# A delta-rule attention block feeding a cosine-gated feed-forward block: the first pair of units inverted by doubling only within blocks of 16, the norms' 1e-6 added on ScalarE, and the whole order of work laid anew

## The chip, the cores and the metric

The kernel runs on one core of one Trainium2 chip. The metric is device time in microseconds (us). The kernel before took 642.42 us, the median of three runs between 641.67 and 646.46 us. One further execution was profiled: it took 642.72 us, and its span from the first to the last instruction is 640.9 us.

## What is computed

For 4 batches and 8 heads, a recurrence runs over 768 positions with a head size of 48. Then a feed-forward block with a cosine gate works on the 3072 tokens.

```python
k_n = k / (np.linalg.norm(k, axis=-1, keepdims=True) + 1e-06)
for t in range(S):
    y[:, :, t] = einsum('bhd,bhde->bhe', q[:, :, t], state)
    v_old = einsum('bhde,bhd->bhe', state, kt)
    state = state + bt * einsum('bhd,bhe->bhde', kt, vt - v_old)
x = y.transpose(0, 2, 1, 3).reshape(B * S, H * D)      # 3072 x 384
h = x @ w_in                                            # 384 x 2048
return (h * np.cos(h)) @ w_out                          # 2048 x 384
```

All numbers are float32, except the two weight matrices, which arrive as float64 and are narrowed on the chip.

## The kernel before

**Units.** The 768 positions are cut into 24 units of 32 positions (C = 32). A unit holds all 32 pairs of batch and head. Two units make a pair (`m = n // 2`), and each pair feeds one step `p` of the feed-forward block with 256 tokens.

**A unit's way through the attention block.** Keys and queries are loaded (`load`, L392) and transposed on TensorE (`turn`, L615; copied out by `turn_out`, L625; later units use a DVE transpose instead). `gram` (L648) makes the products of keys with keys and queries. `gram_keys` (L659) scales them by beta over the squared norm; for that `scale` (L578 to L586) adds 1e-6 to the norm, squares it, takes the reciprocal and multiplies, all on VectorE (DVE). The inverse of the unit's 32x32 triangular matrices is needed before its values can be solved for: `solve` (`p_u`, L935 or L941) multiplies the right side by it, `solve_out` (L953) scales the result, `update` (`p_s`, L966) and `update_out` (L974 or L976) put it into the state, `within` (`p_kq`, L983) and `within_out` (L996) make the unit's output, `features` (`p_z`, L1004) and `features_out` (L1012) turn it into columns of the feed-forward input. The next unit's `through_state` (`p_kq`, L869) and `right_side` (L886) need that state, so the units form one long chain.

**The inverse is made in three ways.**

- Pair 0 (units 0 and 1, `DOUBLED = 2`): the matrix is split into two diagonal blocks of 16 (`near_block`) and the block between them (`OFF`). `double` (L710) inverts the two blocks by repeated squaring in levels 0 to 3, which ends in `Y3`. Levels 4 and 5 then complete the inverse: `Y3` is transposed (L722), multiplied with `OFF` (level 4), copied (L717), multiplied with `Y3` (level 5), and subtracted from `Y3` (L729), which gives `WHOLE`. Each level runs in two halves (`par`) of 16 matmuls of 32x32. `solve` then uses `WHOLE` in one step.
- Pair 1 (`HALVED = 1`): only the two blocks of 16 are inverted, by column steps on GpSimd (POOL) and DVE (`invert`, L818 and L825), after a trip through DRAM (`gram_put` L772, `gram_get` L785, `put` L830, `get` L841). The solve then takes three steps: `solve_half` (`p_w`, L899), `half_out` (ScalarE, ACT, L911), `between` (`p_v`, L899), `between_out` (DVE, L919), `solve` (`p_u`, L935).
- Pairs 2 to 11: the whole matrix by column steps on POOL.

**The feed-forward block.** The weights are narrowed tile by tile: `narrow_load` (L510), `narrow_split` (ACT, L518 and L520), `narrow_shift` (DVE, L524 and L529), `narrow_add` (POOL, L533); tiles 0 to 11 are w_in, 12 to 27 are w_out. Steps p = 0 and 1 use plain products (`hidden`, L1025, eight groups of 24 matmul records per step; `output`, L1223, for p = 0). Later steps use products with fewer multiplications (`layer`, L1199, and `product`, L1281) on sums that DVE and POOL make. The gate is `hidden_turns` (ACT, L1062), `hidden_rest` (DVE, L1069), `hidden_cos` (ACT, L1078), `hidden_gate` (DVE, L1081).

**What sets the order.** Every piece of work is a task (`add`) with its dependencies. `Order.LINE` (L97) is a list of task numbers, and the tasks are issued in just that order, so each engine's queue is a fixed list. `Order.OTHER` (L58) says which tasks go to the other of two engines: loads and stores to ACT's queue instead of SP's (SyncE's), `inv`, `x_sum`, `left` and `right` to DVE instead of POOL or the other way about. A DMA waits until the DMA eight places earlier on the shared list has landed. `keep_warm` (L487) puts matmuls without use into TensorE's list where the list expects it to be idle; 36 of them are in the program.

```python
        for key in line:
            emit, deps, makes, uses = self.tasks[key]
            assert deps <= done, key
            for tag, t in makes:
                self.place[t] = free[tag].pop(0)
            emit()
```

Of the kernel before, what the change touches and what calls it, by code (L numbers as in the profile page):

```python
# [10 lines left out]
FP = mybir.dt.float32  # L11
I32 = mybir.dt.int32
U32 = mybir.dt.uint32
ALU = mybir.AluOpType
# [41 lines left out]
class Order:  # L56

    OTHER = {  # L58
        ('gram_put', 2), ('q', 3), ('gram_get', 1), ('inv', 1, 0), ('put', 1), ('gram_put',
        4), ('gram_put', 5), ('v', 7), ('v', 8), ('v', 9), ('blocks', 11, 1), ('gram_put',  # L60
        11), ('put', 5), ('v', 13), ('put', 6), ('gram_put', 15), ('gram_get', 7), ('get',
        15), ('v', 16), ('blocks', 16, 0), ('blocks', 16, 1), ('gram_put', 16), ('blocks',
        18, 1), ('k', 19), ('blocks', 19, 0), ('gram_get', 9), ('get', 19), ('gram_put',
        20), ('v', 21), ('gram_put', 21), ('put', 10), ('gram_put', 22), ('v', 23),
        ('gram_put', 23), ('gram_get', 11), ('right', 4, 4), ('left', 1, 1, 0), ('left', 1,
        3, 0), ('left', 1, 3, 1), ('store', 1, 0), ('x_sum', 2, 'd'), ('x_sum', 2, 'n'),
        ('x_sum', 2, 'm'), ('x_sum', 2, 'e'), ('x_sum', 2, 'k'), ('x_sum', 2, 'g'),
        ('x_sum', 2, 'i'), ('x_sum', 2, 'l'), ('x_sum', 2, 'f'), ('x_sum', 2, 'b0'),
        ('left', 2, 4, 1), ('left', 2, 3, 1), ('x_sum', 3, 'd'), ('x_sum', 3, 'n'),
        ('x_sum', 3, 'm'), ('x_sum', 3, 'e'), ('x_sum', 3, 'k'), ('x_sum', 3, 'g'),  # L70
        ('x_sum', 3, 'i'), ('x_sum', 3, 'l'), ('x_sum', 3, 'h'), ('x_sum', 3, 'b0'),
        ('left', 3, 4, 1), ('left', 3, 3, 1), ('x_sum', 4, 'd'), ('x_sum', 4, 'm'),
        ('x_sum', 4, 'g'), ('x_sum', 4, 'i'), ('left', 4, 3, 0), ('left', 4, 3, 1),
        ('store', 4, 0), ('x_sum', 5, 'd'), ('x_sum', 5, 'e'), ('x_sum', 5, 'l'), ('x_sum',
        5, 'h'), ('x_sum', 5, 'b0'), ('left', 5, 2, 0), ('left', 5, 4, 1), ('left', 5, 3,
        0), ('left', 5, 3, 1), ('store', 5, 0), ('x_sum', 6, 'd'), ('x_sum', 6, 'g'),
        ('x_sum', 6, 'l'), ('x_sum', 6, 'f'), ('x_sum', 6, 'b0'), ('left', 6, 1, 0),
        ('left', 6, 4, 0), ('store', 6, 1), ('x_sum', 7, 'd'), ('x_sum', 7, 'm'), ('x_sum',
        7, 'g'), ('x_sum', 7, 'i'), ('x_sum', 7, 'f'), ('x_sum', 7, 'h'), ('x_sum', 7,
        'b0'), ('left', 7, 4, 0), ('left', 7, 4, 1), ('left', 7, 3, 1), ('x_sum', 8, 'd'),  # L80
        ('x_sum', 8, 'm'), ('x_sum', 8, 'e'), ('x_sum', 8, 'k'), ('x_sum', 8, 'g'),
        ('x_sum', 8, 'l'), ('left', 8, 3, 0), ('store', 8, 0), ('store', 8, 1), ('x_sum', 9,
        'd'), ('x_sum', 9, 'm'), ('x_sum', 9, 'e'), ('x_sum', 9, 'k'), ('x_sum', 9, 'i'),
        ('x_sum', 9, 'l'), ('x_sum', 9, 'b0'), ('left', 9, 1, 0), ('left', 9, 2, 0),
        ('left', 9, 1, 1), ('left', 9, 3, 0), ('store', 9, 0), ('x_sum', 10, 'k'), ('x_sum',
        10, 'i'), ('x_sum', 10, 'l'), ('x_sum', 10, 'h'), ('x_sum', 10, 'b0'), ('left', 10,
        1, 0), ('left', 10, 1, 1), ('left', 10, 4, 1), ('left', 10, 3, 0), ('left', 10, 3,
        1), ('store', 10, 0), ('x_sum', 11, 'd'), ('x_sum', 11, 'e'), ('x_sum', 11, 'k'),
        ('x_sum', 11, 'g'), ('x_sum', 11, 'f'), ('left', 11, 1, 0), ('left', 11, 2, 0),
        ('left', 11, 1, 1), ('left', 11, 3, 0), ('left', 11, 3, 1), ('store', 11, 1),  # L90
        ('store_right', 11), ('weights', 5), ('weights', 7), ('weights', 15), ('weights',
        16), ('weights', 18), ('weights', 20), ('weights', 22), ('weights', 23), ('weights',
        25), ('weights', 27)
# [142 lines left out]
def kernel(  # L236
# [32 lines left out]
    nc = tc.nc  # L269
# [1605 lines left out]
```

## Time and profile before

| | |
|---|---|
| median of three runs | 642.42 us (641.67 to 646.46) |
| the profiled execution | 642.72 us, span 640.9 us |
| TensorE (PE) busy | 616.0 us, 96% of the span |
| DVE / ACT / POOL busy | 510.5 / 296.4 / 441.5 us |
| PE idle from 106 to 600 us | 1.25 of 494 us |
| PE idle before 106 us | 19.96 of 106 us |

An engine's busy time is the union of its instructions' times. The idle time in the last two rows is the length of the stretch less the busy time in it. One matmul of the program shows as two matmul records and two weight loads in the trace, since its numbers are float32. A wait of an engine is put down to what ended last; "issue" means that nothing in the profile explains it. Line numbers are those of the kernel before; the changed kernel's lines lie up to 17 further down.

### The profile page before, as it was taken

To read this page: it belongs to the slowest core of one execution; us is meant where nothing else is said; L and a number is where in the kernel's file an instruction comes from. 1 tells how busy PE (TensorE), PEld (TensorE's weight loads), DVE (VectorE), ACT (ScalarE), POOL (GpSimd) and SP (SyncE) were. 2 spreads that over 40 slices of the span, in tenths; PEclk is the share of its full clock that TensorE was granted. 3 is DMA by queue.
4 is the path that set the end of the run, shared out by engine and by line. 5 is a ranking of instruction groups with operands and counts; after the bars stand their busy time and mean duration, and the time that the engine had idled before them with its cause. 6 is when DMAs were issued, how large, how long until landed. Compare 5 with 4: busy or idle time off the path is not lost.

```text
span 640.9 us, 25243 instructions
## 1 busy us (share of the span) xinstructions
PE 616.0 (96%) x10688; PEld 570.7 (89%) x10688; DVE 510.5 (80%) x1049; ACT 296.4 (46%) x528; POOL 441.5 (69%) x780
## 2 busy tenths in 40 slices
PE   5877999999999999999999999999999999999997
PEld 4655877897799999999999999999999999999997
DVE  5776877998989899887898888888888786656682
ACT  3444655654334453553642544643643553545440
POOL 5435888888778788788689888886883884112231
PEclk9887999999999999999999999999999999999999
DMA  9777556563551454434536245243304202000000
GB/s 189 200 177 180 113 157 145 93 141 54 100 88 20 98 87 70 86 69 73 88 68 104 49 70 99 49 67 67 74 2 78 45 3 41 19 2 26 2 25 26
DMA packets 209369, 50.38 MB, mean 79 GB/s; under 512 B 200920, under 2 KB 204264, under 8 KB 209256
## 3 DMA queue, kind: packets, MB, share of 16 engines
q1 hardware_dynamic: 161896, 35.03, 28.7%
q10 hardware_dynamic: 47072, 13.25, 10.1%
q8 instruction: 84, 1.38, 0.9%
q0 software_dynamic: 288, 0.50, 0.4%
q14 instruction: 29, 0.24, 0.1%
HBM read 38.51 MB, written 10.22 MB: 76 GB/s over the span
## 4 chain that ended last, share of the span: by engine, by line
PE 82%; DMA 7%; DVE 4%; issue 2%; SPq 2%; POOL 1%; ACT 1%; ACTq 0%; DVEq 0%; POOLq 0%
PE p_out L1281 28%; PE p_h L1199 27%; PE p_h L1025 6%; PE p_out L1223 3%; PE p_kq L869 3%; PE p_s L966 3%; PE p_kq L983 3%; DMA kp<-in_k_dram 3%; PE p_u L941 2%; PE p_g L648 2%; PE p_h L1281 2%; PE p_z L1004 1%; DMA g_ffn<-in_moe_w_in_dram 1%; SPq L392 1%; DMA z_dr<-z 1%
## 5 line engine op out<-in xcount | busy, mean ns | idle before, releaser
L818 POOL TENSOR_TENSOR part<-z,gb 128x126 f32<-128x126 f32 (+23 forms) x321 | 146.1, 455 | 41.8 <-DMA gb<-g_dr 12.9
L825 POOL TENSOR_TENSOR z<-z,part 128x126 f32<-128x126 f32 (+23 forms) x321 | 146.9, 458 | 25.1
L1281 PE MATMUL p_out<-w_out,g_ffn 128*128 128x192 f32 x672 | 121.9, 329 | 0.6 <-DVE o L1333 0.6
L1281 PEld LDWEIGHTS p_out<-w_out,g_ffn 128*128 128x128 f32 x672 | 107.7, 190 | 2.0 <-DVE o L1333 0.9
L1078 ACT ACTIVATE turns<-turns,halfpi 128x512 f32<-128x512 f32 x96 | 68.0, 718 | 55.0 <-DVE turns L1069 43.0
L1281 PE MATMUL p_out<-w_sum,g_ffn 128*128 128x192 f32 x496 | 89.7, 329 | 0.2 <-DVE o L1333 0.2
L1199 PE MATMUL p_h<-x_sum,w_in 128*128 128x128 f32 x640 | 84.0, 277 | 0.0
L1062 ACT ACTIVATE turns<-g_ffn,quarter_turn 128x512 int32<-128x512 f32 x70 | 49.8, 719 | 66.7 <-DVE g_ffn L1216 29.5
L1281 PEld LDWEIGHTS p_out<-w_sum,g_ffn 128*128 128x128 f32 x496 | 79.6, 190 | 1.2 <-issue 0.4
L1199 PEld LDWEIGHTS p_h<-x_sum,w_in 128*128 128x128 f32 x640 | 78.8, 192 | 1.1
L1216 DVE TENSOR_TENSOR g_ffn<-g_ffn,p_h 128x512 f32<-128x512 f32 x80 | 54.2, 680 | 17.3 <-PE p_h L1199 16.4
L1069 DVE SCALAR_TENSOR_TENSOR turns<-g_ffn,turns 128x512 f32<-128x512 f32 x70 | 54.3, 783 | 13.0 <-ACT turns L1062 12.9
L996 ACT COPY y<-p_kq 32x384 f32<-32x384 f32 x96 | 45.1, 470 | 36.4 <-PE p_kq L983 30.0
L1081 DVE TENSOR_TENSOR g_ffn<-turns,g_ffn 128x512 f32<-128x512 f32 x70 | 51.9, 751 | 3.8 <-ACT turns L1078 3.7
L567 POOL TENSOR_TENSOR knrm<-ksum,halves 128x16 f32<-128x16 f32 (+1 forms) x14 | 38.4, 2745 | 22.8 <-DVE ksum L555 20.7
L1199 PE MATMUL p_h<-x_sum,in_sum 128*128 128x128 f32 x400 | 52.9, 277 | 0.0
L1199 PEld LDWEIGHTS p_h<-x_sum,in_sum 128*128 128x128 f32 x400 | 49.7, 192 | 0.8
L1333 DVE SCALAR_TENSOR_TENSOR o<-p_out,o 128x192 f32<-128x192 f32 x74 | 25.1, 351 | 29.3 <-PE p_out L1281 28.8
L1025 PE MATMUL p_h<-x_ffn,w_in 128*128 128x128 f32 x384 | 46.1, 277 | 0.0
L1025 PEld LDWEIGHTS p_h<-x_ffn,w_in 128*128 128x128 f32 x384 | 44.2, 192 | 1.4 <-issue 0.2
L1199 PE MATMUL p_h<-x_ffn,w_in 128*128 128x128 f32 x320 | 42.4, 277 | 0.0
L1297 POOL TENSOR_TENSOR g_ffn<-g_ffn,g_ffn 128x512 f32<-128x512 f32 x18 | 25.4, 1417 | 23.2 <-PE p_out L1281 19.4
(156 smaller groups left out, 1080.8 us busy)
## 6 DMA issues: line engine op xcount, KB each, us to landing
g_ffn<-in_moe_w_in_dram SPq DMA_DIRECT2D x10, 512.0 KB
gb<-g_dr SPq DMA_DIRECT2D x14, 256.0 KB
vp<-in_v_dram SPq DMA_DIRECT2D x68, 48.0 KB
g_ffn<-in_moe_w_out_dram SPq DMA_DIRECT2D x8, 384.0 KB
g_ffn<-in_moe_w_out_dram ACTq DMA_DIRECT2D x8, 384.0 KB
kp<-in_k_dram SPq DMA_DIRECT2D x120, 24.0 KB
out_dram<-o SPq DMA_DIRECT2D x14, 192.0 KB
zt<-z_dr SPq DMA_DIRECT2D x72, 32.0 KB
```

Of the source, the lines that this page charges most:

```text
L567: nc.gpsimd.tensor_tensor(out=scales[m][2][:, part], in0=sums[m, part.start][:, 0:n], in1=halves[:, 0:n], op=ALU.pow,)
L818: eng.tensor_tensor(out=part, in0=z[:, 0:rows, j, None].to_broadcast(shape), in1=a[:, j, None, j + 1 :].to_broadcast(shape), op=ALU.mult,)
L825: eng.tensor_tensor(out=behind, in0=behind, in1=part, op=ALU.subtract)
L996: nc.scalar.copy(by_parity(y[quarter(b)]), p_kq[quarter(b ^ 1), :, b % 2])
L1025: nc.tensor.matmul(p_h[:, i], w_in[:, t, (4 * k + i) * 128 : (4 * k + i + 1) * 128], xts[p][:, t, unit * 128 : (unit + 1) * 128], start=(i ...
L1062: nc.scalar.activation(turns[p, f], hidden_of(p, f), AF.Identity, bias=quarter_turn, scale=TURN)
L1069: nc.vector.scalar_tensor_tensor(out=r, in0=hidden_of(p, f), scalar=TURN, in1=t, op0=ALU.mult, op1=ALU.subtract,)
L1078: nc.scalar.activation(r, r, AF.Sin, bias=halfpi, scale=2.0 * math.pi)
L1081: nc.vector.tensor_tensor(out=place(p, f), in0=step_of(rests.pop((p, f)), f), in1=step_of(hidden_of(p, f), f), op=ALU.mult,)
L1199: nc.tensor.matmul(p_h[:, e], in_block(*w)[:, e], x_of(p, b), start=new and e == 0, stop=True, skip_group_check=True,)
L1216: nc.vector.tensor_tensor(out=part_of(p, to), in0=part_of(p, one), in1=part_of(p, two), op=op)
L1281: nc.tensor.matmul(p_o, left(p, part, a)[:, e % 4], right(e, b), start=(e == 0), stop=(e == FT // 2 - 1), skip_group_check=True,)
```

## The change

1. `COMPLETED = ()`: no doubled unit is completed any more. Units 0 and 1 skip levels 4 and 5 and the transpose of `Y3`, and are solved in the three steps of pair 1, with `Y3` as the inverse of the blocks and `OFF` between them.
2. `scale` loses its first two DVE instructions. A new function `norms_near` makes the squared norm plus 1e-6 and the norm plus 1e-6 on ACT, between POOL's root and DVE's reciprocal.
3. `LINE` and `OTHER` are new from end to end: each queue's order is another, some loads and stores change queue, and the last three of pair 1's block columns (`inv`, 1, 3) go from POOL to DVE.

```diff
+    COMPLETED = ()
-    tiny = const.tile([128, 2, H], FP, name="tiny")
+    tiny = const.tile([128, 1], FP, name="tiny")
...
+    def norms_near(m, part):
+        knrm = scales[m][2][:, part]
+        krec = krecs[m, part.start] = work.tile([128, 2, H], FP, name="krec")[
+            :, 0 : part.stop - part.start
+        ]
+        nc.scalar.activation(krec, knrm, AF.Square, bias=tiny)
+        nc.scalar.activation(knrm, knrm, AF.Identity, bias=tiny)
...
     def scale(m, part):
-        bs, bz, knrm = (t[:, part] for t in scales[m])
-        nc.vector.tensor_tensor(out=knrm, in0=knrm, in1=tiny[:, 0:n], op=ALU.add)
-        krec = work.tile([128, 2, H], FP, name="krec")[:, 0:n]
-        nc.vector.tensor_tensor(out=krec, in0=knrm, in1=knrm, op=ALU.mult)
+        bs, bz = (t[:, part] for t in scales[m][0:2])
+        krec = krecs.pop((m, part.start))
         nc.vector.reciprocal(krec, krec)
...
+    def blocks_of(n):
+        return power(n)[:, WHOLE if n in COMPLETED else Y3]
+
     def solve_half(n):
-        triangular(n, "p_w", zts[n], rhss[n])
+        triangular(n, "p_w", blocks_of(n) if n < DOUBLED else zts[n], rhss[n])
...
     def between(n):
-        triangular(n, "p_v", off_blocks[n], first.pop(n))
+        triangular(
+            n, "p_v", power(n)[:, OFF] if n < DOUBLED else off_blocks[n], first.pop(n)
+        )
...
     def solve(n):
-        zt, rhs = power(n)[:, WHOLE] if n < DOUBLED else zts.pop(n), rhss.pop(n)
+        zt, rhs = blocks_of(n) if n < DOUBLED else zts.pop(n), rhss.pop(n)
...
-        for level in range(len(LEVELS)):
+        for level in range(len(LEVELS) if n in COMPLETED else 4):
...
-                if level == 3:
+                if level == 3 and n in COMPLETED:
...
+            add(("near", m, a), "ACT", 0.5, lambda: norms_near(m, part), [("norms", m, a)])
-            add(("scale", m, a), "DVE", 1.1, lambda: scale(m, part),
-                [("norms", m, a), ("beta",) if n < PLAIN_TURNS else ("beta_home",)])
+            add(("scale", m, a), "DVE", 0.65, lambda: scale(m, part),
+                [("near", m, a), ("beta",) if n < PLAIN_TURNS else ("beta_home",)])
...
-        if m == HALVED:
+        three = m == HALVED or n < DOUBLED and n not in COMPLETED
+        if three:
```

The part of the built order that the prediction speaks of, TensorE's list of the changed kernel around the first solves (matmuls of the program, the lines are the changed kernel's):

```
33 L625 Matmult p_t<-consts,kp_101 128x128 x4
34 L625 Matmult p_t<-consts,qp_103 128x128 x4
35 L909 Matmult p_w<-vp,in_sum 32x48 x32
36 L489 Matmult p_out<-o_93 128x256
37 L720 Matmult p_h_70<-w_sum 32x2x32 x16
38 L909 Matmult p_v<-g_ffn_77,in_sum 32x48 x32
39 L489 Matmult p_out<-o_93 128x256
40 L950 Matmult p_u<-g_ffn_77,in_sum 32x48 x32
...
53 L1040 Matmult p_h_70<-x_ffn,w_in 128x128 x12
54 L658 Matmult p_g<-kq_t 32x64 x32
55 L489 Matmult p_out<-o_93 128x256
56 L1040 Matmult p_h_69<-x_ffn,w_in 128x128 x12
57 L909 Matmult p_w<-rhs,w_sum 32x48 x32
...
70 L1040 Matmult p_h_71<-x_ffn,w_in 128x128 x12
71 L909 Matmult p_w<-rhs,w_sum 32x48 x32
72 L909 Matmult p_v<-g_ffn_75,in_sum 32x48 x32
73 L489 Matmult p_out<-o_93 128x256
74 L950 Matmult p_u<-g_ffn_75,w_sum 32x48 x32
75 L981 Matmult p_s<-u,kp_100 64x96 x16
```

and ACT's list between the transposes of unit 4 (`kq_t`) and the copy of unit 0's first step (`g_ffn_77<-p_w`):

```
42 L394 DMACopy qp_103<-in_q_dram 32x8x48 x4
43 L512 DMACopy g_ffn_78<-in_moe_w_in_dram 128x1024
44 L635 TensorCopy kq_t<-p_t 128x2x2x4x32 x2
45 L520 Activation w_in<-g_ffn_76 128x512
46 L522 Activation g_ffn_76<-g_ffn_76 128x512
47 L924 TensorCopy g_ffn_77<-p_w 128x2x4x48
```

More of the change, by code (lines that the diff above doesn't have):

```diff
@@ L58 @@
     OTHER = {
[L59 to L70, printed above, removed]
@@ L89 @@
[L89 to L93, printed above, removed]
+        ('k', 3), ('inv', 1, 0), ('inv', 1, 3), ('gram_put', 4), ('q', 5), ('q', 6), ('k',
+        7), ('get', 7), ('v', 8), ('gram_put', 8), ('v', 9), ('blocks', 9, 0), ('blocks',
@@ new lines @@
+        10, 0), ('blocks', 10, 1), ('gram_put', 10), ('blocks', 11, 0), ('blocks', 11, 1),
+        ('gram_put', 12), ('blocks', 13, 0), ('put', 6), ('gram_put', 15), ('gram_get', 7),
+        ('gram_put', 16), ('gram_put', 17), ('gram_get', 8), ('blocks', 18, 1), ('gram_put',
+        18), ('get', 18), ('v', 19), ('v', 21), ('v', 22), ('blocks', 22, 1), ('store', 0,
+        1), ('right', 3, 4), ('right', 3, 6), ('left', 1, 3, 0), ('store', 1, 1), ('x_sum',
+        2, 'd'), ('x_sum', 2, 'n'), ('x_sum', 2, 'm'), ('x_sum', 2, 'e'), ('x_sum', 2, 'k'),
@@ new lines @@
+        ('left', 4, 3, 1), ('x_sum', 5, 'n'), ('x_sum', 5, 'g'), ('x_sum', 5, 'i'),
+        ('x_sum', 5, 'l'), ('x_sum', 5, 'b0'), ('left', 5, 4, 1), ('left', 5, 3, 0),
+        ('left', 5, 3, 1), ('x_sum', 6, 'n'), ('x_sum', 6, 'k'), ('x_sum', 6, 'i'),
+        ('x_sum', 6, 'l'), ('x_sum', 6, 'b0'), ('left', 6, 4, 1), ('left', 6, 3, 0),
+        ('left', 6, 3, 1), ('x_sum', 7, 'd'), ('x_sum', 7, 'n'), ('x_sum', 7, 'm'),
+        ('x_sum', 7, 'e'), ('x_sum', 7, 'k'), ('x_sum', 7, 'i'), ('x_sum', 7, 'l'),
@@ L1518, in unit @@
             ready, makes=[("two", ("p_u", n))],
-            uses=[("rhs", n) if n else ("vp", m)] + ([] if n < DOUBLED else
-                  [("u_half", n)] if m == HALVED else [("zt", n)]))
+            uses=[("rhs", n) if n else ("vp", m)] + ([("u_half", n)] if three else
+                  [] if n < DOUBLED else [("zt", n)]))
         add(("solve_out", n), "DVE", 1.12, lambda: solve_out(n), [("solve", n), scaled],
```

41 lines of the change are left out of this document (23 added, 18 removed), and 200 rows, old and new, of the table LINE.

## The prediction

> **What bounds the kernel now.** I read, in this order, the busy time by stretches, TensorE's timeline from the start, the DVE and ACT timelines beside it, and the built order of both kernels. Busy time of each engine in six stretches of the span:
>
> ```profile
> 0.00:47.00 47.00, 35.76 (x924) 26.61 (x924) 33.41 (x100) 19.30 (x40) 20.07 (x25) 0.89 0.83 184
> 47.00:64.00 17.00, 12.23 (x434) 9.38 (x433) 11.19 (x31) 8.47 (x19) 10.41 (x13) 0.80 0.73 194
> 64.00:91.00 27.00, 24.43 (x684) 21.17 (x666) 23.00 (x46) 18.30 (x37) 22.73 (x38) 1.00 0.65 153
> 91.00:106.00 15.00, 13.62 (x478) 12.33 (x477) 9.99 (x18) 7.50 (x15) 12.77 (x24) 1.00 0.43 91
> 106.00:600.00 494.00, 492.75 (x7959) 464.56 (x7948) 410.28 (x817) 231.18 (x402) 364.75 (x676) 1.00 0.36 65
> ```
>
> Columns: stretch, length, then busy us of PE, its weight loads, DVE, ACT, POOL, then PE's granted clock, DMA share and GB/s. From 106 us on PE is idle 1.25 of 494 us: there the list of matmuls is the time, and it is the same list in both kernels (5412 matmuls; 128 of 32x32 in levels 4 and 5 go, 128 of 32x48 in `p_w` and `p_v` come). So nothing can be won after 106 us, only lost. Before it PE is idle 19.96 us and also runs 36 warming matmuls. Those are waits for the chain of units 0 to 3:
>
> ```profile
> 47.76 0.78 PE L935 MATMUL p_u<-vp,in_sum 32*32 32x48 f32 x53 [0.73 <-ACT kq_t L625]
> 51.24 0.31 PE L935 MATMUL p_u<-vp,in_sum 32*32 32x48 f32 x10 [2.70 <-issue]
> ...
> 64.12 3.25 PE L1025 MATMUL p_h<-x_ffn,w_in 128*128 128x128 f32 x24
> ...
> 69.06 0.88 PE L935 MATMUL p_u<-rhs,w_sum 32*32 32x48 f32 x64
> ...
> 87.96 0.28 PE L935 MATMUL p_u<-g_ffn,w_sum 32*32 32x48 f32 x4 [1.28 <-issue]
> 88.17 2.94 PE L1025 MATMUL p_h<-x_ffn,w_in 128*128 128x128 f32 x24
> 91.04 0.89 PE L966 MATMUL p_s<-u,kp 64*64 64x96 f32 x32
> ```
>
> Columns: start, length, instruction, count, idle time before it and what ended it. Unit 0 is solved at 47.8 to 51.5, unit 1 at 69.1, unit 2 at 85.8 to 88.2; `u` of these ends on DVE at 52.65, 71.02 and 89.29. The first feed-forward group starts at 64.1.
>
> **The change, part by part.**
>
> *Levels 4 and 5 against three steps.* On DVE `Y3` of unit 0 ends at 36.6 (L729 at 36.33, 0.28) and `WHOLE` at 46.06 (two adds from 45.58). So 9.5 us of chain go. In their place stand `p_w` 0.88, its copy 0.48, `p_v` 0.88 and the subtraction 0.54 = 2.8 us (rows L899, L911, L919 of unit 2). If all else were ready, `u` of unit 0 would come 6.7 us sooner. Unit 1 loses more: its right side was ready at 63.6 (L886 from 62.20) and waited 5.4 us for its inverse. The matmuls cost PE nothing net: eight groups of 0.45 go, four of 0.88 come.
>
> *What is late next for unit 0* is the load order. In the new list `p_t` of unit 4 stands before `p_w` of unit 0, and needs `k4`. Ahead of it go 12 unit loads of 0.197 MB (4 x 48 KB), 6 weight tiles of 0.524 MB and about 0.5 MB of constants: 6.0 MB at the 184 GB/s of the first row is 32.7 us, and with a landing of 4 us (the chain has one of 4.01 at 35.64) `p_t` runs near 36 and `p_w` near 37. ACT's copy of `p_w` stands behind the load of tile 7, which waits for a piece of `k5` (another 0.77 MB, 4.2 us: about 39), a `kq_t` copy of 1.07 and a split of 1.3: 41.4. Then copy 0.5, `p_v` 0.9, subtraction 0.6, `p_u` 0.9, `u` 1.0 and 1.3 for a gap as below: 46.6, that is 6 us sooner. Without the hold on ACT it would be 42; with landings of 7.2 (the chain's weight tile at 23.85) instead of 4, 50.
>
> *Gaps in short matmuls.* Six PE gaps are put to "issue" before 91 us (16.47, 29.45, 35.12, 44.73, 51.24, 87.96: 0.93 to 2.70 us, 9.3 in all). Counted in matmuls and weight loads they stand at 451, 962, 1219, 1730, 1986 and 4034, multiples of 256 apart, and the instruction queue moved 84 packets and 1.38 MB, 16.4 KB each. So they are instruction blocks that came late beside the loads. The new list puts such borders into `p_v` of unit 0 and `p_u` of unit 2; before they lay in `p_u` of units 0 and 2. I take 1.3 for each, between nothing and 2.7. The Trainium skill (Runtime: NRT & Kernel Launch, Instruction fetch mechanics) states the block of 256 instructions, which agrees with the spacing, and that crossing it is "mostly hidden". By that rule the sum would be about 1.3 us lower; the gaps of 2.70 and 1.28 in the solves speak against it.
>
> *The norms.* 28 DVE instructions of 0.17 go (4.8 us, 5 of the 14 pairs of them before 91 us), 28 on ACT come. ACT shows none of 128x8; the nearest are 0.20 (128x1, L454) and 0.27 (128x128, L717), so 5.6 to 7.6 us on an engine that is busy 46%. One reason excludes a price after 106 us: PE does not wait there. At the start it costs: ACT's two for unit 0 stand behind four issues of `k3` at 0.45 each, an issue of tile 1 and two squares, so `bs` comes near 15.5 instead of 11.95. This 3.5 us is hidden by the wait for `k4`: four levels need to end only by 37. Without that cover it would cost up to 3.5.
>
> *Unit 1.* From `u` of unit 0 (46.6): update, `within` and the copies of `y` took 6.3 (52.65 to 58.93), so 52.9; then on PE `p_kq` 1.1, three warming matmuls 1.3, `p_t` 1.1, level 3 0.5, a feed-forward group 2.9, `p_g` 0.8, a warming one 0.4, a second group 2.8, `p_w` 0.9: 64.7. Three steps more (0.5, 0.9, 0.6, 0.9) and `u` 1.0: 68.6 to 69 against 71.0. Only 2 us, but with one more feed-forward group (2.7) behind it.
>
> *Unit 2.* Pair 1's last columns go from POOL (ended 69.36) to DVE behind the first `turns` work, near 62; its way to DRAM and back took 69.4 to about 80 and moves from ACT's queue to SP's, behind the loads of w_out, so about 73. That is not last any more. `u` of unit 1 (69), update 0.9, `within` 0.8 with a warming one 0.4, `y` 1.9, `p_kq` 1.1, warming one 0.4, `p_z` 0.4, a group 2.7, `p_w` 0.9, then ACT's copy behind an `x_ffn` copy, four splits and two cosines (about 1.5 late), 0.5, `p_v` 0.9, 0.6, `p_u` 0.9 plus 1.3, `u` 1.0: 84.5 at `p_s`, against 91.0.
>
> *The sum.* 6.5 us sooner at `p_s` of unit 2, less what the new list has not yet done by then: one feed-forward group (2.7) and one `p_t` of eight (1.1). That is 2.7. From there the new list has work without a break, where the old one lost 1.4 idle and 0.4 warming until 106: I give it all of that and no such loss of its own, +1.8. 2.7 + 1.8 = 4.5, so 642.72 - 4.5 = 638.2 for an execution like the profiled one. That one lies 0.3 above the median of the runs: 637.9.
>
> *The order after 106 us.* Moved work: 11 loads of v, 8 of k, gathers and stores between SP and ACT, some sums between DVE and POOL. PE's changes between large and small matmuls number 130 there instead of 128 at about 0.1 us: nothing. A new wait costs what the few old ones did, 0.35 to 0.65 (such as 0.39 at 257.8).
>
> **The rivals.**
>
> - *The chain is not held on ACT.* `p_w`'s copy comes at once (u of unit 0 at 42) and unit 1 and 2 keep the 4.5 us. Speaks for it: in the old trace the loads up to `k5` had landed by 40. Against: `kq_t` and split stand there in any case. Time 638 - 4.5 = 633.5.
> - *The front gain is given back.* The weight tiles, not the units, feed PE up to 106: POOL's last w_in add is at 76.8 and ACT's w_out loads run until 105, DMA is 65% busy from 64 to 91. Then PE is full at the old time: 642.5.
> - *Slower: the units come too soon in the list.* From unit 2 on, each update stands 2 to 6 us of PE work earlier in the new list. If POOL starts pair 2's columns no sooner than now (85.75), `p_u` of units 4 and 5 stops PE until they are there. Each us by which POOL starts later than about 81 costs one; a start at 92 gives 642.7 - 4.5 + 11 = 649. For it: POOL is 84% busy from 64 to 91. Against: its inputs, `p_g` of units 4 and 5, move with the chain.
> - *ACT's table.* The two new functions could make ACT reload its table: the trace has one such load, of 1283 ns (L454). Twice for each of 14 pairs would be 36 us beside ACT's 296, and late scales at the start: about 2 us given back, 640. Against it: one load serves squares, copies and sines in the old trace, and the built change still holds one. The Trainium skill (ScalarE activation tables: per-element evaluation and per-set limits, Table sets in the compiler and the runtime) has the back end place these loads by runs of instructions, which leaves both open. I give it 0.02.
>
> **How the numbers follow.** Forecast (a gain of 2 to 7, 635.5 to 641) 0.43, held chain free 0.23, given back 0.17, too soon in the list 0.15, table 0.02. The range leaves out 0.1 at each end: down to 631, past the first rival with the gap of unit 0 hidden, up to 647, most of the slower one. The likeliest case's own range is 635.5 to 641. One per cent is 6.4 us, which is about what a measurement of this kernel can tell from no change. Under 636.0: the free chain and a sliver of the forecast, 0.31. Over 648.8: part of the slower rival, 0.09. Between: 0.60.
>
> **What would show it.** Right: `p_u` of unit 0 on PE near 45 and its `u` at 45 to 48; `p_w` of unit 0 released by `p_t`, not by `Y3`; the copy of `p_w` on ACT with a DMA issue before it; `u` of unit 1 near 69, `p_s` of unit 2 near 84.5; PE idle 12 to 16 us before 106 and 1 to 2 after; gaps put to "issue" in `p_v` of unit 0. Wrong: `bs` of unit 0 on the chain, PE idle over 4 us after 106, POOL's columns of pair 2 starting after 83, or PE waiting for weight adds between 85 and 106.

## The result and the profile after

The changed kernel takes 649.97 us, the median of 18 runs (643.38 to 651.61), against 643.18 us for the kernel before (18 runs, 639.08 to 646.46). The ratio is 1.0084 with a 95% interval of 1.0062 to 1.0107: slower by 5.4 us, where 637.9 was forecast, and past the top of the range (647.0). The medians lie 6.8 us apart; the ratio is nearer to that of the means (648.6 and 643.1), since the runs of the changed kernel lie in two groups (643.4 to 647.9 and 649.9 to 651.6). The change is inside one per cent, but it is clear of the noise.

The profiled execution took 645.07 us with a span of 643.3, which is 2.35 more than the old one's 642.72. It is the second shortest of the 18 runs, so what it shows is not what the median run lost (see the account, below). Busy time by stretches of this execution; the last two rows are stretches of half clock (length, then PE, PEld, DVE, ACT, POOL, clock, DMA share, GB/s):

```profile
0.00:47.00 47.00, 35.15 (x882) 26.79 (x882) 28.02 (x86) 22.83 (x51) 19.76 (x25) 0.85 0.81 178
47.00:64.00 17.00, 16.89 (x445) 13.98 (x445) 14.14 (x37) 8.53 (x17) 12.15 (x20) 0.91 0.71 192
64.00:91.00 27.00, 23.10 (x767) 18.65 (x766) 20.79 (x41) 16.07 (x33) 17.62 (x21) 0.87 0.64 146
91.00:106.00 15.00, 13.61 (x385) 11.54 (x383) 10.39 (x22) 8.08 (x17) 13.35 (x27) 1.00 0.52 110
106.00:600.00 494.00, 492.87 (x7976) 464.58 (x7965) 405.27 (x799) 234.92 (x419) 365.09 (x675) 1.00 0.38 65
...
39.00:50.00 11.00, 9.05 (x235) 6.57 (x239) 3.33 (x6) 4.93 (x9) 5.36 (x4) 0.53 0.72 156
70.50:77.00 6.50, 6.42 (x108) 4.10 (x102) 4.30 (x9) 0.98 (x3) 2.64 (x3) 0.50 0.70 149
```

PE's idle time before 106 us fell from 19.96 to 17.25 us, but from 64 to 91 us it rose from 2.57 to 3.90, and the clock there fell from 1.00 to 0.87. TensorE's timeline shows the solves of units 0 to 2 and the start of unit 3's:

```profile
40.32 1.50 PE L909 MATMUL p_w<-vp,in_sum 32*32 32x48 f32 x64 [3.49 <-ACT kq_t L635]
45.39 0.85 PE L909 MATMUL p_v<-g_ffn,in_sum 32*32 32x48 f32 x29 [0.63 <-issue]
47.33 1.50 PE L950 MATMUL p_u<-g_ffn,in_sum 32*32 32x48 f32 x64
...
66.01 0.88 PE L909 MATMUL p_w<-rhs,w_sum 32*32 32x48 f32 x64
67.55 0.88 PE L909 MATMUL p_v<-g_ffn,w_sum 32*32 32x48 f32 x64 [0.65 <-ACT g_ffn L924]
69.67 0.89 PE L950 MATMUL p_u<-g_ffn,w_sum 32*32 32x48 f32 x64 [1.24 <-DVE g_ffn L934]
...
88.54 1.14 PE L981 MATMUL p_s<-u,kp 64*64 64x96 f32 x32 [1.24 <-DVE u L968]
...
105.28 0.88 PE L950 MATMUL p_u<-g_ffn,w_sum 32*32 32x48 f32 x64 [0.73 <-DVE g_ffn L934]
...
108.96 0.89 PE L981 MATMUL p_s<-u,kp 64*64 64x96 f32 x32
```

Unit 0 is solved at 47.33, where 47.76 to 51.5 stood before; unit 1 at 69.67 (69.06 before); unit 2's update comes at 88.54 (91.04 before); unit 3's `p_u` at 105.28, against 105.22 in the old trace. The same solve matmuls took 1.50 instead of 0.88 where the clock was halved.

At the end, SyncE's last four issues in the old kernel and in the changed one (ACT's four run beside them):

```profile
635.31 3.12 SPq L1351 DMA_DIRECT2D out_dram<-o  x4
```

```profile
638.91 1.74 SPq L1366 DMA_DIRECT2D out_dram<-o  x4
```

In the new list `store` (11, 1) stands behind `store_right` (11), which waits for the last sum on DVE (638.53). So all eight last issues come after it, where four of eight used to go ahead. From the start of the last matmul to the end of the span it is 5.1 us instead of 4.0.

So of this execution's 2.35 us, 1.1 lie at the end, and by an estimate 1.1 were lost by 106 us and 0.2 between. The 1.1 at 106 us are estimated from the work left: one feed-forward group less done (2.7) and 8 `p_t` records more to do (1.0), against 8 records of `p_out` already done (2.6), at an equal place of unit 3.

### The profile page after: what moved, and what is told of

Read it like the earlier page. It is cut to its first block, busy times and chain, and to the rows that moved or that the text cites. A ratio compares the mean times of both kernels' runs of the same rounds, so it can differ in the third digit from the quotient of the medians.

```text
span 643.3 us, 25175 instructions
## 1 busy us (share of the span) xinstructions
PE 620.1 (96%) x10688; PEld 573.7 (89%) x10688; DVE 502.1 (78%) x1023; ACT 302.1 (47%) x554; POOL 437.4 (68%) x772
## 4 chain that ended last, share of the span: by engine, by line
PE 86%; DMA 4%; POOL 3%; DVE 3%; issue 1%; ACT 1%; SPq 1%; ACTq 0%; DVEq 0%; POOLq 0%
PE p_out L1296 30%; PE p_h L1214 29%; PE p_h L1040 5%; PE p_kq L879 4%; DMA kp<-in_k_dram 3%; PE p_s L981 3%; PE p_out L1238 3%; PE p_kq L998 3%; PE p_g L658 2%; PE p_u L956 2%; PE p_h L1296 2%; PE p_out L489 1%; PE p_z L1019 1%; POOL z L835 1%; POOL part L828 1%
## 5 line engine op out<-in xcount | busy, mean ns | idle before, releaser
L828 POOL TENSOR_TENSOR part<-z,gb 128x126 f32<-128x126 f32 (+24 forms) x318 | 142.3, 448 | 36.2 <-DMA gb<-g_dr 8.4
L835 POOL TENSOR_TENSOR z<-z,part 128x126 f32<-128x126 f32 (+24 forms) x318 | 147.8, 465 | 24.9
L1214 PE MATMUL p_h<-x_sum,w_in 128*128 128x128 f32 x640 | 82.2, 277 | 0.6 <-ACT p_h L1226 0.6
L1214 PEld LDWEIGHTS p_h<-x_sum,w_in 128*128 128x128 f32 x640 | 77.4, 192 | 1.5 <-ACT p_h L1226 0.8
L1312 POOL TENSOR_TENSOR g_ffn<-g_ffn 128x512 f32<-128x512 f32 x16 | 22.2, 1389 | 53.2 <-DVE g_ffn L1096 49.1
L1226 ACT COPY p_h<-p_h 128x512 f32<-128x512 f32 x40 | 23.0, 575 | 49.7 <-PE p_h L1214 23.4
L1040 PE MATMUL p_h<-x_ffn,w_in 128*128 128x128 f32 x384 | 46.1, 278 | 0.0
```

The lines of the kernel that those rows point to most:

```text
L828: eng.tensor_tensor(out=part, in0=z[:, 0:rows, j, None].to_broadcast(shape), in1=a[:, j, None, j + 1 :].to_broadcast(shape), op=ALU.mult,)
L835: eng.tensor_tensor(out=behind, in0=behind, in1=part, op=ALU.subtract)
L1040: nc.tensor.matmul(p_h[:, i], w_in[:, t, (4 * k + i) * 128 : (4 * k + i + 1) * 128], xts[p][:, t, unit * 128 : (unit + 1) * 128], start=(i ...
L1214: nc.tensor.matmul(p_h[:, e], in_block(*w)[:, e], x_of(p, b), start=new and e == 0, stop=True, skip_group_check=True,)
```

## The experiments

`LINE` is quoted by the tasks' names, not by their numbers. Ratios are to the kernel before, run beside each, with 95% intervals.

**A second trace (again).** The changed kernel unaltered.

> The changed kernel unaltered, for a second trace: its executions lie in two groups, near 645 and near 650 us, and the first trace is one of the first group. Theory 1 (the clock): in an execution near 650 TensorE's granted clock is halved once or twice more before 106 us, for 6 to 7 us each time, and TensorE idles under 2 us after 106. Theory 2 (a late transfer or a late inverse): the clock is as in the first trace and TensorE idles 4 to 6 us at one place after 106 us. If this execution lies near 645 as well, it tells nothing of the two.

It took 652.48 us (one run, span 650.7). ACT's and PE's timelines around unit 3:

```profile
99.92 0.36 ACTq L512 DMA_DIRECT2D g_ffn<-in_moe_w_out_dram  x1
105.17 0.54 ACT L520 ACTIVATE w_out<-g_ffn 128x384 f32<-128x384 f32 x1 [3.83 <-DMA g_ffn<-in_moe_w_out_dram]
106.05 0.46 ACT L924 COPY g_ffn<-p_w 128x384 f32<-128x384 f32 x1
```

```profile
106.57 0.88 PE L909 MATMUL p_v<-g_ffn,in_sum 32*32 32x48 f32 x64 [2.69 <-ACT g_ffn L924]
108.38 1.50 PE L950 MATMUL p_u<-g_ffn,w_sum 32*32 32x48 f32 x64 [0.93 <-DVE g_ffn L934]
113.64 0.89 PE L981 MATMUL p_s<-u,kp 64*64 64x96 f32 x32
...
287.18 1.16 PE L1214 MATMUL p_h<-x_ffn,in_sum 128*128 128x128 f32 x8 [2.18 <-DVE g_ffn L1231]
```

ACT's list has a weight split ahead of unit 3's copy; the tile landed late, so the copy, and PE behind it, waited, and the clock halved (`p_u` 1.50). Unit 3's update came 4.7 us later than in the first trace (108.96), and a further 2.7 us were lost from there to the last matmul, nearly all of it at 287. Two places of this order therefore cost something or nothing, by when a DMA lands. One trace did not show that.

**The last store (tail).**

```diff
-('store_right', 11), ('store', 11, 1)
+('store', 11, 1), ('collect', 11, 3), ..., ('store_right', 11)
```

> The changed kernel with one task moved: the last store of whole rows stands ahead of the last collected product, as in the kernel before. In the first trace of the changed kernel all eight last DMA issues (four on SP, four on ACT) start after DVE's last sum, and the span ends 5.1 us after TensorE's last matmul; in the kernel before four of the eight start 2.3 us before that sum, and the span ends 4.0 us after the matmul. Theory 1: the last two issues of each queue are the end, so this gains 0.9 to 1.3 us. Theory 2: the last landing sets the end and the issues ahead of it are hidden: nothing.

649.19 us, 1.0088 [1.0054, 1.0122]. The end of the span came 4.0 us after the start of the last matmul instead of 5.1, as expected, but the median did not show it. Its trace has the loss near 280 us that the changed kernel's second trace had. DVE and PE:

```profile
277.46 1.42 DVE L645 STREAM_TRANSPOSE kq_t<-qp 128x256 f32<-128x256 f32 x4 [2.95 <-DMA qp<-in_k_dram]
```

```profile
279.51 1.98 PE L1214 MATMUL p_h<-x_ffn,in_sum 128*128 128x128 f32 x8 [2.15 <-DVE g_ffn L1231]
281.28 1.91 PE L1214 MATMUL p_h<-x_ffn,w_in 128*128 128x128 f32 x8
282.99 1.09 PE L1214 MATMUL p_h<-x_sum,in_sum 128*128 128x128 f32 x8
```

The load is `blocks` (15, 0). In the old list it stands 81 tasks ahead of its user, `turn_out` (15); in the new one 13 tasks ahead, on SP behind the eight loads of `k` (17). It lands late, DVE waits 2.95 in its list, the sums behind it are late, PE waits 2.15, and then runs at half clock for 3.4 us (1.98 and 1.91 where 1.09 follows). In the first trace of the changed kernel the same load landed in time. Over the traces of this and the later runs: with the load at its new place PE waits 2.06 to 2.34 us there in five of eight (again, tail, start_mended, filled, completed), and with the load moved back in none of six (late_mended, both_mended, best, two_places, start_two, start_two_norms).

**Warming (warm).** Seventeen warming matmuls without use moved (not the 20 of the expectation; the trace holds 34 more matmul records, two for each): four ahead of `p_g` of unit 0, seven ahead of its `p_w`, three into unit 1's steps, one into unit 2's and two behind it.

```diff
+('warm', ...) x7, ('solve_half', 0)
+('warm', ...), ('between', 1), ..., ('warm', ...) x2, ('solve', 1)
```

> The changed kernel with 20 of its warming matmuls that have no place any more (those behind the first real product emit nothing) moved to where TensorE idles: 4 before the first products of keys, 7 before the first step of unit 0's solve, 1 and 2 between the steps of unit 1's, 1 between those of unit 2's and 2 behind it. Theory 1 (the clock): the idle places halve the granted clock, at 9 to 15, 40 to 50 and 70.5 to 77 us of the first trace; with them filled these stretches run at full clock, unit 0's values come 3 us sooner (near 47), the last of 18 us at half speed becomes under 6, and the time falls by 3 to 6 us and scatters less. Theory 2 (the order alone): the clock follows the waits but costs nothing, since DVE's and ACT's lists set the chain; the time stays within 1 us.

649.57 us, 1.0107 [1.0062, 1.0151]. The windows show that the edit did its work:

```profile
39.00:50.00 11.00, 8.63 (x256) 6.57 (x255) 6.26 (x10) 4.87 (x9) 6.57 (x4) 1.00 0.80 169
```

The granted clock from 39 to 50 us is 1.00 instead of 0.53, and 70 to 78 us ran at full clock too. The time did not fall, though the interval is wide: a gain of up to some 2 us against the changed kernel would fit it, the 3 to 6 us of theory 1 would not. Nor does the run test the clock alone. `p_w` of unit 0 started at 43.35, straight behind the warming matmuls (40.23 to 43.42) and 1.8 us after the copy `kq_t` had freed its buffers (41.51), so the filling itself held the step. Whether the half clock there costs anything is left open.

**Three steps in the old order (old_order).** The kernel before, with three steps, and ACT's norms directly behind each root.

```diff
-('double', n, 4, .), ('double', n, 5, .), ...
+('norms', m, a), ('near', m, a)
+('solve_half', n), ('half_out', n), ('between', n), ('between_out', n)
```

> The three-step solve of units 0 and 1 and the norms on ScalarE alone, in the order of the kernel before: the four tasks of the three steps stand where the last two levels of the inverse stood, each norm task directly behind its root, unit 4's products of keys behind unit 1's solve, everything else as before. Theory 1: the change of the computation gains at the start what the chain allows (unit 0's values near 47 to 50, unit 2's update 0 to 3 us sooner) and 639 to 643 us come out; what makes the changed kernel slower is its new order. Theory 2: the three steps themselves cost (more short dependent products, more idle between them, so a lower clock): 645 to 650 us, as the changed kernel.

661.64 us, 1.0291 [1.0256, 1.0325]. It tells nothing of the three steps: the transposes of unit 4 held unit 0's update to 55.6 us, and the norms stood at a bad place (below, before_norms).

**Late places, start, both, norms (late_mended, start_mended, both_mended, norms_dve).**

```diff
 late_mended:
+('store', 11, 1), ('collect', 11, 3)
+('blocks', 15, 0), ('k', 17)
+('half_out', 3), ('split', 20), ('split', 22)
 start_mended:
+('state', 1), ('turn', 4), ('turn_out', 4)
+('half_out', 0), ('split', 6)
-OTHER: ('weights', 7), ('inv', 1, 3)
 norms_dve, scale:
-        nc.scalar.activation(krec, knrm, AF.Square, bias=tiny)
-        nc.scalar.activation(knrm, knrm, AF.Identity, bias=tiny)
+        nc.vector.tensor_tensor(out=knrm, in0=knrm, in1=tiny[:, 0:n], op=ALU.add)
+        nc.vector.tensor_tensor(out=krec, in0=knrm, in1=knrm, op=ALU.mult)
```

> The changed kernel with three things of its new order after 95 us mended: the last store of whole rows ahead of the last sum; the load of unit 15's first transposed block ahead of the eight loads of pair 8's k on SP, since in two of three traces DVE's transposes wait 2.95 us for it near 280 us and TensorE then 2.2; ACT's splits of weight tiles 20 and 22 behind the copy between unit 3's steps, since in the second trace that copy stood behind a split that waited 3.8 us for its tile, and TensorE 2.7 us for the copy. Theory A (the new order's late places cost): 1.1 + 2 + up to 2, so 645 to 647 against some 650. Theory B (only the start costs, what is lost later is slack): 648 to 650.

648.36 us, 1.0083 [1.0051, 1.0115]: nothing won. Two of the three edits removed their waits; the third made a new one. DVE and PE at unit 3:

```profile
103.89 0.64 DVE L526 SCALAR_TENSOR_TENSOR g_ffn<-g_ffn 128x384 uint32<-128x384 uint32 x1 [3.39 <-ACT g_ffn L522]
```

```profile
106.17 1.50 PE L950 MATMUL p_u<-g_ffn,w_sum 32*32 32x48 f32 x64 [3.14 <-DVE g_ffn L934]
```

With the split moved behind the copy, DVE's shift of that tile waits 3.39 us for it, and `between_out` stands behind the shift. PE waits 3.14 here instead of 2.69 one step earlier. both_mended, which has the same edit, shows the same wait (2.81). That it takes back what the other two edits win is likely, but the trace alone does not show it: two_places, without this edit, has its update of unit 3 just as late in its own trace (112.76 against 112.62).

> The changed kernel with its start mended: unit 4's transposes behind unit 1's right side instead of ahead of unit 0's solve (their buffer and k4's landing held the first step until 40.3 us), the load of tile 7 issued by SP instead of ACT, split 6 behind unit 0's copy, and the last three of pair 1's columns back on POOL (on DVE they stood ahead of unit 1's last subtraction, which came 1.2 us late). Theory A: unit 0's values come at 43 to 45 us instead of 49.9, unit 1's 1 to 3 us sooner, and 2 to 4 us are won, 646 to 648. Theory B (the weights and POOL's columns set what TensorE can do before 106 us): unit 0 comes sooner and the time does not move, 649 to 651.

647.24 us, 1.0055 [1.0029, 1.0081]: a gain of 0.0029 on the changed kernel, 1.9 us (the intervals overlap). `p_w` of unit 0 starts at 37.45 instead of 40.32 and its `p_u` at 44.70 instead of 47.33, so PE's step had indeed waited for unit 4's transposes.

> Both of these mends. Theory A: they add up, 641 to 644, no slower than the kernel before. Theory B: as the one with only the late places mended.

646.77 us, 1.0055 [1.003, 1.0079]: with the third late edit inside, as start_mended alone.

> The changed kernel with the norms' two instructions back on DVE (the tasks on ScalarE are empty), order kept. If the move to ScalarE costs nothing, as forecast, the time stays within 1 us of the changed kernel's and DVE is busy 4 to 5 us longer. If ScalarE's two instructions are what comes late at the start, where they stand behind DMA issues and squares, the scales of unit 0 come 1 us sooner and 1 to 3 us are won.

647.46 us, 1.0062 [1.0037, 1.0088]. The norms back on DVE are worth 0.0022, 1.4 us; the interval overlaps that of the changed kernel.

**PE work put between the steps (filled), and the old order once more (best, old_order2).** `best` is filled with start_mended's edits, the store and the load. `old_order2` moves unit 4's transposes out of unit 0's way and unit 1's steps together.

```diff
 filled:
+('solve', 2), ('hidden', 0, 6)
+('right', 3), ('solve_half', 3)
+('between', 3), ('hidden', 0, 10)
 old_order2, on old_order:
+('state', 1), ('turn', 4), ('turn_out', 4), ('right', 1), ('solve_half', 1)
```

> The changed kernel with three groups of TensorE's work at units 2 and 3 in another place, nothing else: one feed-forward group stands between unit 2's solve and its update, and two stand between the three steps of unit 3's solve, instead of behind them. In all traces of the changed kernel TensorE idles 1.23 us in the first place and 0.65 and 0.73 or more in the second, where the kernel before idles too in the second; in three of six traces the granted clock halves between 102 and 113 us for 3.4 to 6.8 us, in which every matmul takes half as long again or twice as long. Theory C (these short waits, and the half clock that follows them while TensorE is full, make the longer group of executions): the waits go, the clock stays full from 90 us on, 2.6 us come for sure and 2 to 3 more in the longer executions: 644 to 646 instead of 650, with less scatter. Theory D (POOL's columns or the weights set the time at 106 us): what is won here is lost again before 140 us: 649 to 651.

650.43 us, 1.0139 [1.0098, 1.018], the wrong way (the intervals overlap). PE's timeline shows the cover missing elsewhere:

```profile
90.67 0.55 PE L1019 MATMUL p_z<-consts,y 128*128 128x128 f32 x3 [2.14 <-ACT y L1011]
...
100.12 1.21 PE L909 MATMUL p_w<-rhs,w_sum 32*32 32x48 f32 x64 [1.87 <-DVE rhs L896]
```

A group moved to cover one wait uncovers another, here of 2.14 and 1.87, each followed by half clock (91 to 95, 101 to 105 us).

> The same three groups moved, with the mended start, the last store and unit 15's block load as in the runs before (the splits of tiles 20 and 22 in their old place, since behind the copy they let DVE's shift of tile 22 hold unit 3's last subtraction). Theory C: the parts add up: 650 less 1 to 2 (start), 1.1 (store), 2 to 4 (load and the half clock behind it), 3 to 5 (the groups): 638 to 643, no slower than the kernel before. Theory D: 645 to 647, as with both mends alone.

649.18 us, 1.0118 [1.0079, 1.0157]: not what its parts promised. The same edits without the three groups give 1.0021 (start_two, below), so there the groups lose about 6 us (the intervals do not meet).

> The three steps and the norms on ScalarE in the order of the kernel before, placed anew, since in the first such run (661) the transposes of unit 4 stood between unit 0's values and its update and held it for 4.7 us, and unit 1's solve stood behind a feed-forward group. Here the update follows the values at once, unit 4's transposes follow unit 1's state, unit 1's first step stands ahead of the feed-forward group. If the three steps themselves gain and the first run lost by its places: unit 0's update near 51, unit 1's before 70, 640 to 645. If the three steps cost by themselves (their short waits, a lower clock): 650 and more again.

678.93 us, 1.0574 [1.0536, 1.0611]: my placement by hand made it much worse; nothing follows for the change.

**The two late places alone, with the start, with the norms; the old computation in the new order (two_places, start_two, start_two_norms, completed).**

```diff
 two_places:
+('store', 11, 1), ('collect', 11, 3)
+('blocks', 15, 0), ('k', 17)
 start_two: two_places and start_mended
 start_two_norms: start_two and norms_dve
 completed:
-    COMPLETED = ()
+    COMPLETED = (0, 1)
-('solve_half', n), ('half_out', n), ('between', n), ('between_out', n)
+('double', n, 4, .), ('double_copy', n, 4, .), ('double', n, 5, .), ('double_add', n, 5, .)
```

> The changed kernel with only the last store ahead of the last sum and unit 15's block load ahead of pair 8's k. Theory E (two late places after 106 us make most of the loss: 1.1 us at the end, and near 280 us 2.2 us of wait with often 1.7 more of half clock behind it): 650 less 3.3 to 5, 645 to 647. Theory F (the start makes it): 648.5 to 650.

644.0 us, 1.0036 [1.0013, 1.006]: 0.0048 less than the changed kernel, 3.1 us; the intervals do not meet, if only just (1.0060 and 1.0062). Unit 3's wait is still in its trace, which is of the one long execution of its 12 (648.44; the others end by 645.4):

```profile
104.54 0.92 PE L909 MATMUL p_v<-g_ffn,in_sum 32*32 32x48 f32 x64 [2.62 <-ACT g_ffn L924]
```

> The mended start with the same two. Theory E: 647 less 3 to 4: 643 to 644.5, equal to the kernel before within the interval. Theory F: 645.5 to 647.

643.96 us, 1.0021 [0.9997, 1.0044]: the start adds 0.0015, 1.0 us, inside the noise.

> As start_two, with the norms' two instructions back on DVE. If ScalarE's share of the chain at the start is what remains, 1 to 2 us less than start_two; if they cost nothing there, the same within 1 us.

642.18 us, 0.9991 [0.9968, 1.0013]: the best version, as fast as the kernel before. With the norms on DVE another 0.0030, 1.9 us.

> The new order with the old computation: levels 4 and 5 complete both inverses where the new order has the first two steps of the solves (the two halves of unit 1's last level one behind the other, one feed-forward group two places later, for want of a buffer). If the three steps gain in this order, as forecast for the start, this is 1 to 4 us slower than the changed kernel: 651 to 654. If the solve is not what the start waits for, it is the same: 649 to 651. If the three steps lose, 646 to 648.

651.68 us, 1.0139 [1.0101, 1.0177]. With levels 4 and 5 back, the new order is 0.0055 or 3.5 us slower than with three steps, but the intervals overlap (from 1.0101 to 1.0107). The trace does not show the gain at the start, where it should arise: unit 3's update comes at 109.90, and the changed kernel's own traces have it from 106.04 to 113.64. The load near 280 is late in it (PE idle 2.23), and one feed-forward group had to move. That the three steps gain in the new order is therefore likely, not settled.

**The same two causes put into the kernel before (before_norms, before_late).**

```diff
 before_norms:
-    COMPLETED = ()
+    COMPLETED = (0, 1)
+('norms', m, a), ('near', m, a)      (every pair, in before's LINE)
 before_late:
+('store_right', 11), ('store', 11, 1)
+('k', 19), ('blocks', 15, 0)
```

> The kernel before with the norms' two instructions on ScalarE, each pair directly behind its root in ScalarE's list, and nothing else of the change. If the move costs by itself, as the two runs with it undone hint: 1 to 3 us slower, a ratio of 1.002 to 1.005. If it costs nothing, as forecast: within 1 us, a ratio of 0.9985 to 1.0015.

655.08 us, 1.0204 [1.0166, 1.0243]. ACT and PE:

```profile
351.62 0.31 ACT L581 ACTIVATE krec<-knrm,tiny 128x16 f32<-128x16 f32 x1 [9.93 <-POOL knrm L569]
```

```profile
353.41 1.60 PE L1214 MATMUL p_h<-x_sum,in_sum 128*128 128x128 f32 x8 [3.60 <-ACT p_h L1226]
```

The price is not ACT's 0.31 us but the wait in its list: POOL's root comes up to 9.93 us later than ACT reaches the instruction, the copies of `p_h` stand behind it, and PE waits. PE shows waits of the same size in old_order (near 226, 359 and 363 us) and old_order2 (near 244, 377 and 380). The new order puts these tasks later in ACT's list and has one such wait, 1.64 at 21.99 us. So this run shows what the placement can cost, not what it costs in the change.

> The kernel before with the two late places put in and nothing else: the last store of whole rows behind the one that waits for the last sum, and the load of unit 15's first transposed block behind pair 9's k on SP, ten tasks ahead of its transposes instead of 81. Theory E: the store costs 1.1 us and the load 0 to 4, by how late it lands: a ratio of 1.002 to 1.008. If these places are slack here: 0.9985 to 1.001.

646.35 us, 1.0049 [1.0022, 1.0077]: the two places cost the kernel before 3.1 us, as much as taking them out gave the changed one. DVE and PE (the row names another DMA as what ended the wait; the load that the transposes read is issued from 285.85 on, behind the eight loads of `k`, where the kernel before issued it at 270.35):

```profile
291.34 1.42 DVE L635 STREAM_TRANSPOSE kq_t<-qp 128x256 f32<-128x256 f32 x4 [2.35 <-DMA g_dr<-g]
```

```profile
293.22 0.85 PE L648 MATMUL p_g<-kq_t 48*32 48x64 f32 x64 [1.31 <-DVE tt L754]
```

**The three steps alone in the old order (old_three).** Norms on DVE, unit 0's steps behind its right side, unit 1's around the first feed-forward group.

```diff
+('right', 0), ('solve_half', 0), ..., ('solve_out', 0), ('update', 0), ('update_out', 0)
+('right', 1), ('solve_half', 1), ('half_out', 1), ('hidden', 0, 0), ('between', 1), ...
```

> The three steps of units 0 and 1 alone in the order of the kernel before, the norms on DVE as before: unit 0's steps, its update and its state straight behind its right side, unit 1's first step ahead of the first feed-forward group, unit 4's products of keys behind unit 1's update. If the three steps gain in the old order too, unit 0's values come near 48 instead of 52.65 us, unit 1's near 69, and a ratio of 0.992 to 1.000 comes out. If they lose there, 1.003 and more. With the 13 us of the norms' place and the 5 us by which unit 4's transposes held unit 0's update taken off the first run (661), 643 is what the sum gives.

654.55 us, 1.0198 [1.0155, 1.0241]. Unit 0's update came 4.9 us sooner (47.9 against 52.8), but my list lost it at once:

```profile
65.05 1.57 PE L911 MATMUL p_w<-rhs,w_sum 32*32 32x48 f32 x64 [3.01 <-DVE rhs L898]
```

Unit 1's update was at 74.2 (71.2 before) and unit 2's first step at 90.6 (82.6). What three steps are worth in the old order stays open.

## Why the prediction was wrong

**What came as forecast.** `bs` of unit 0 at 14.4 (15.5), `p_t` of unit 4 at 35.77 (36), the copy of `p_w` on ACT behind the issue of tile 7 at 41.97 (41.4), the gap put to "issue" in unit 0's `p_v` (0.63, where 1.3 was taken), no second table load, PE idle 1.13 us after 106 (1 to 2) in the first trace. PE's idle time before 106 was not as forecast: 17.25, and not 12 to 16.

**Step "What is late next for unit 0": 3.3 us too early.** `u` ended at 49.9 instead of 46.6. ACT's timeline:

```profile
38.79 0.36 ACTq L512 DMA_DIRECT2D g_ffn<-in_moe_w_in_dram  x1
39.19 1.07 ACT L635 COPY kq_t<-p_t 128x512 f32<-128x512 f32 x2 [5.04 <-DMA kp<-in_k_dram]
40.15 0.68 ACT L520 ACTIVATE w_in<-g_ffn 128x512 f32<-128x512 f32 x1
...
41.97 0.48 ACT L924 COPY g_ffn<-p_w 128x384 f32<-128x384 f32 x1 [0.57 <-PE p_w L909]
```

The hold on ACT was seen, and the copy of `p_w` came only 0.6 later than forecast (41.97). What was not seen: `p_w` shares its buffers in PSUM, TensorE's output memory, with `p_t` (the tag `two` in the kernel), so PE's step itself waits for the `kq_t` copy (40.32, 3.49 idle), and half clock follows the idle time, from 39.7 to 49.9 us. The other 2.7 us came behind the copy: PE ran its short matmuls at 1.50 instead of 0.88 there, and the warming matmul and the products of level 3 that stand between `p_w` and `p_v` in its list (1.22 and 1.08) were no term of the sum. In the other three traces with this list up to unit 3, `u` ended at 47.5 to 48.7 (again, tail, two_places), so 1 to 2 us too early is nearer to the usual run.

**Step "Unit 1": 2.6 us too early** (71.6 instead of 69). DVE's timeline:

```profile
66.55 0.68 DVE L1084 SCALAR_TENSOR_TENSOR turns<-p_h,turns 128x512 f32<-128x512 f32 x1
67.15 0.90 DVE L828 TENSOR_TENSOR part<-z,gb 128x39 f32<-128x39 f32 x1
...
68.98 0.19 DVE L835 TENSOR_TENSOR z<-z,part 128x15 f32<-128x15 f32 x1
69.07 0.55 DVE L934 TENSOR_TENSOR g_ffn<-rhs,p_v 128x384 f32<-128x384 f32 x1
```

Of these, 2.2 us were there before the steps: `p_w` ended at 66.89, not 64.7, since unit 0 was late. The steps add the rest: `between_out` stands behind the columns that the change moved from POOL to DVE, and behind `turns`, and starts 0.64 us after `p_v` is done (68.43). The sum costed only where these columns end, not who queues behind them. PE then idles 0.65 and 1.24 within 3 us, and half clock follows from 70.5 to 77.

**Step "The sum" failed in both terms.** The terms given for unit 2 add up to 85.2 at its `p_s`, not 84.5, so the lead forecast was 5.8 by its own terms. Measured it was 2.5 us (88.54 against 91.04); less the 2.7 and 1.0 not yet done that is -1.2, where +2.7 stood. (In the other three traces the lead was 2.3, 4.1 and 5.4.) And the +1.8 for "work without a break" did not come: the new list idled as well (1.24 at 88.54, then 0.65 and 0.73), and unit 3's `p_u` stood where it did before (105.28 against 105.22). So the front gives back the gain, as the second rival said, in this trace through waits of the steps. In again and two_places a weight tile does take part: it lands late, ACT's split waits 3.8 us for it, and the copy between unit 3's steps stands behind the split.

**Step "The order after 106 us" failed most.** It took "nothing", and 0.35 to 0.65 for a new wait. Two moved DMAs cost 3.1 us, shown twice: taken out (two_places, 1.0084 to 1.0036) and put into the kernel before (before_late, 1.0049). PE's idle time after 106 us was the forecast's test, and the first trace met it only because its load landed in time: the second trace has 5.0 us there and tail 3.4. The prediction compared PE's list and did not ask how far each load stands ahead of its user, nor which wait stands ahead of the last store.

**"The norms" were costed at nothing.** Going back is worth 1.4 us (norms_dve) and 1.9 (start_two_norms); each pair's intervals overlap, so it is likely and not settled. How the placement in the new order would cost it is not shown.

**The slower rival had the sign right by luck, not the mechanism.** POOL started pair 2's columns at 87.48, past the point (about 81) from which the rival should decide. But they ended at 122.5 and `p_u` of unit 4 came at 135.4: PE never waited for them.

**The account.** From the ratios, 5.4 us = two late places 3.1, norms 1.4 to 1.9, the start 1.0 to 1.9; these add up to 5.5 to 6.9, and start_two_norms, which mends all three, stands at 0.9991. Only the two places are clear of the noise by themselves. The start and the norms are so at most together (1.0036 to 0.9991, 2.9 us; the intervals meet at 1.0013). The account is not closed: start_two_norms still has the three steps, and if these win the 3.5 us of completed, about as much is lost elsewhere in the new order, at a place that no run names.

**Why the runs lie in two groups.** Four traces have the same list up to unit 3's update, and the same work from there on:

| trace | unit 3's update | from there to the last matmul | from there to the end |
|---|---|---|---|
| the first (645.07) | 108.96 | 529.2 | 5.1 |
| again (652.48) | 113.64 | 531.9 | 5.1 |
| tail (645.31) | 106.04 | 533.5 | 4.0 |
| two_places (648.44) | 112.76 | 529.9 | 4.0 |

The one list reaches unit 3's update within a range of 7.6 us; the two late ones are those in which the weight tile landed late. The second column is longer by 2.7 and 4.2 us in the two in which the load near 280 landed late. So much of a run's time hangs on which of two transfers land late, and a single trace can show either, both or none: the front of the first trace is no measure of the median run. That the groups are just these cases is likely, but four traces do not settle it. Even the fastest of these fronts wins little. Tail's update of unit 3 is 5.4 us ahead of the old trace's (111.49), but the old one needs only 525.4 us from there to its last matmul, against 529.2: 1.7 us are left, where 4.5 were forecast.

## What to carry to other kernels

When a whole order is new, compare for each load how far it stands ahead of its user and what is queued ahead of it, and for each store which wait it stands behind: here two places cost 3.1 us. Cost a step that is moved to another engine by what it waits for there and who is queued behind it, not by its own 0.3 us. Take a second trace before trusting a "no new wait": here one list reached the same matmul up to 7.6 us apart.

## What the runs showed of the hardware

In these traces half clock followed idle times of 0.65 and 1.24 us within 3 us (67 to 70 us of the changed kernel), one wait of 2.15 (tail), and waits of 2.14 and 1.87 (filled). It does not always follow: in again a wait of 2.18 at 287 us left the clock at 1.00. Half clock lasted 3.4, 6.8 or 10.2 us in the changed kernel's traces. The Trainium skill (TensorE: Matmul & The Clock Gate, Part 1: The HAM clock gate) describes two states, decided over windows of about 3.4 us; the two clocks (0.50 and 1.00) and the lengths agree. Its advice (Why this matters for your kernels) to avoid gaps over about 3 us is too wide for this kernel by these numbers.

A wait can therefore cost more than its length, where PE has work without a break. The same late load shows both cases: against the first trace, again lost 2.7 us from unit 3's update to the last matmul, with 2.18 us of idle time and no half clock there; tail lost 4.2, with 2.15 us of idle time and 3.4 us of half clock behind it.
